# Two parts of a weight matrix requested from ScalarE's queue instead of SyncE's, in a block attention and gated MLP kernel

## The chip, the cores and the metric

The kernel runs on one core of a Trainium2 chip. A core has five engines that run side by side and meet through semaphores: TensorE (PE in the profile, PEld for its weight loads), VectorE (DVE), ScalarE (ACT), GpSimd (POOL) and SyncE (SP, here a pure issuer of transfers). The metric is the device time of one execution in microseconds. The kernel before took 508.56 us (median of 3 runs, 508.21 to 508.85).

## The reference, cut to what matters

```python
# block attention: B, H, S, D = 8, 8, 576, 64, in chunks of 64 positions
scores = scale * np.matmul(q_c, k_c.transpose(0, 1, 2, 4, 3))
scores = scores - np.max(scores, axis=-1, keepdims=True)
attn = np.exp(scores)
attn = attn / (np.sum(attn, axis=-1, keepdims=True) + 1e-09)
out = np.matmul(attn, v_c)
# gated MLP on x of [8, 576, 512]; w_in is [512, 1024], w_sg [576, 576], w_out [512, 512]
h = gelu_tanh(x @ w_in)
u, v = h[..., :512], h[..., 512:]
v_n = (v - mean(v)) / sqrt(var(v) + 1e-6) * g_ln
v_s = np.einsum('ts,bsd->btd', w_sg, v_n) + b_sg[None, :, None]
return x + (u * v_s) @ w_out
```

The weights `w_in` and `w_out` reach the kernel as 64-bit floating point words, and each is split on the chip into a high and a low part for the matrix products.

## The kernel before, in words

The 4,608 tokens are cut into 36 tiles of 128. For each tile the attention runs in three steps: S (scores on PE, maximum on DVE, exponentials on ACT, normalisation), T (transposition) and O (the product with v). The MLP then runs by batch element in units: v (the second half of w_in, gelu, the normalisation), u (the first half of w_in), s (w_sg), o (w_out). Each product is three matmuls of high and low parts.

The start is a list written out by hand, `START`. Its first steps are `L0 A0 L1 A1 L2 L3 A4 W0 S0 W1 D8 w0 S1 W2 T0 w1 ...`. L is `v_w_load`, the request of one of the four parts of w_in's second half (512 KB each, called `wsg_106`, `wsg_111`, `wout_115` and `wout_117` by the tiles whose memory they borrow). A requests attention tiles up to that number: tile 0 in two transfers, q and k together (512 KB) and v (256 KB), the later ones in one of 768 KB. W and w are the two halves of a part's conversion into high and low. W (`pair_begin`) is an absolute value on ACT (L130), then steps on DVE (L131, L132, L133, L162, L166). w (`pair_end`) is a negated copy to `win_h` on ACT (L174), five matmuls on PE (L178), which take the identity matrix `ident` and two scaled copies of it, `low`, as operands, and a copy to `win_l` on ACT (L179). D8 (`keep_clock`) is eight matmuls of `ident` with itself whose result nobody reads; each stands in the profile as two records. `ident` is cast on ACT (L103) from `eye`, which GpSimd makes, and the two `low` tiles are made from `eye` on ACT (L108).

The list is not the order on an engine. The framework schedules: it gives each engine one fixed order of its instructions, worked out from its own assumed durations, and on the chip each engine runs this order, waiting at each instruction until its operands are there. A transfer that an engine requests stands in that engine's order as well.

Lines of the kernel before that the prediction names: L291 and L292 request tile 0, L200 and L206 parts of w_in, L314 are the scores, L333 and L340 the maximum and its scaling, L344 tile 0's eight exponentials by head, L355 to L358 the normalisation, L366 the transposition, L398 the product with v, L97 a low part on DVE or GpSimd, L452 the v unit's matmuls, L577 those of D8. Behind the changed place the lines of the changed kernel have numbers one higher.

Of the kernel before, what the change touches and what calls it, by code (L numbers as in the profile page):

```python
# [25 lines left out]
DH = DF // 2  # L26
# [54 lines left out]
def block_attention_gated_mlp(ctx: ExitStack, tc: tile.TileContext, qkv, w_in, w_out, w_sg, g_ln, b_sg, out):  # L81
    nc = tc.nc
# [99 lines left out]
    def w_out_tile(i, dt=F32R):  # L182
        return const.tile([P, KT * DM], dt, name=f"wout_{i}", tag=f"wout_{i}")

    def w_sg_tile(i, dt=F32R):
        return const.tile([P, 5 * S], dt, name=f"wsg_{i}", tag=f"wsg_{i}")
# [10 lines left out]

    def v_w_load(kt):
        st = staged["v", kt] = w_sg_tile(kt, I32) if kt < 2 else w_out_tile(kt - 2, I32)
        nc.sync.dma_start(out=st[:, : 2 * DH], in_=w_in[:, kt, 2 * DH :])  # L200

    def u_w_load(dt):

# [351 lines left out]
    def att_slots(b, n):  # L555
# [9 lines left out]

    steps = {
        "L": v_w_load, "M": lambda k: load_misc(), "W": v_w_begin, "w": v_w_end, "X": u_w_begin, "x": u_w_end, "A": ahead,
        "S": att_scores, "T": att_transpose, "O": att_out, "P": lambda t: att_scores(t, t + 1), "Q": lambda t: att_out(t, t + 1),
    }
# [67 lines left out]
```

## Time and profile before

| what | value |
|---|---|
| median of 3 runs | 508.56 us |
| the profiled execution, its own time | 508.83 us |
| its span, first to last instruction | 507.0 us |
| granted clock of TensorE, mean | 0.998 |
| PE busy | 494.4 us (97%) |
| DVE busy | 339.1 us (67%) |
| ACT busy | 274.7 us (54%) |
| first matmul starts | 5.80 us |

The times of instructions count from the first instruction of the span. The time of an execution is 1.8 us more than the span. Busy time of PE is modelled from pipelined matmuls; a busy PE isn't PE at its peak. In a row of the timeline stand the start, the duration, the engine, the line, the operation, what it writes and reads, and in brackets how long the engine had been idle and what ended this. SPq and ACTq are the engines' issuing of transfers.

### The profile page before, as it was taken

The page shows a single profiled execution, that of the slowest core. Times are in us where ns is not written, and L with a number is a line of the kernel's source. Part 1 is how long each engine was busy: PE and PEld are TensorE (multiplying, and loading weights), DVE is VectorE, ACT ScalarE, POOL GpSimd, SP SyncE. Part 2 cuts the span into 40 slices and gives each one's busy share as a digit, 9 for nine tenths or more (in the row PEclk, how much of TensorE's full clock was granted, in tenths as well). Part 3 has the DMA queues.
Part 4 walks back from the last instruction along what each step waited for, and adds up shares of the span by engine and source line. Part 5 has one row for each costly group of instructions (what it writes and reads, how often), then busy time and mean ns, then how long its engine had stood idle before and what let it go on. Part 6 is the DMA issues. An engine that isn't in the chain of part 4 may idle for free.

```text
span 507.0 us, 12386 instructions
## 1 busy us (share of the span) xinstructions
PE 494.4 (97%) x5244; PEld 458.1 (90%) x5244; DVE 339.1 (67%) x707; ACT 274.7 (54%) x509; POOL 69.9 (14%) x72
## 2 busy tenths in 40 slices
PE   5999999999999999999999999999999999999996
PEld 4667898799999899989999899999999899999996
DVE  7998779888856947586563866576565676536141
ACT  5899667753445764355642775355643766334210
POOL 0112100210211401022100321022100141002000
PEclk9999999999999999999999999999999999999999
DMA  8948010228167204241324204060415200010002
GB/s 335 326 136 234 3 35 25 69 78 207 34 186 227 64 11 117 86 134 39 89 66 154 63 1 127 37 183 2 125 26 170 87 1 4 25 71 0 1 1 93
DMA packets 49595, 46.58 MB, mean 92 GB/s; under 512 B 35202, under 2 KB 39554, under 8 KB 49540
## 3 DMA queue, kind: packets, MB, share of 16 engines
q1 hardware_dynamic: 49540, 45.80, 30.3%
q8 instruction: 41, 0.67, 0.6%
q14 instruction: 14, 0.11, 0.1%
HBM read 36.34 MB, written 9.44 MB: 90 GB/s over the span
## 4 chain that ended last, share of the span: by engine, by line
PE 88%; DVE 6%; ACT 4%; DMA 1%; issue 1%; POOL 0%; DVEq 0%; SPq 0%; ACTq 0%
PE pm L509 21%; PE pm L489 20%; PE pm L532 19%; PE pm L452 18%; PE banks L322 3%; PE pm L410 3%; PE pm L178 2%; ACT pt L344 1%; DMA qkv_t<-qkv 1%; PE pm L314 1%; PE pm L577 1%; DVE gl L97 1%; DVE gt L513 1%; ACT L455 1%; DVE blocks L372 1%
## 5 line engine op out<-in xcount | busy, mean ns | idle before, releaser
L509 PE MATMUL pm<-wsg,v 128*128 128x288 f32 x768 | 107.9, 296 | 0.0
L509 PEld LDWEIGHTS pm<-wsg,v 128*128 128x128 f32 x768 | 103.9, 189 | 0.3
L532 PE MATMUL pm<-gh,wout 128*128 128x288 f32 x512 | 92.3, 297 | 0.0
L532 PEld LDWEIGHTS pm<-gh,wout 128*128 128x128 f32 x512 | 76.1, 189 | 0.5
L461 POOL TENSOR_TENSOR sm<-sm,neg_half 128x1 f32<-128x1 f32 x36 | 36.5, 1013 | 165.6 <-DVE sm L460 165.6
L358 POOL TENSOR_TENSOR pt<-pt,den 128x512 f32<-128x512 f32 x27 | 29.7, 1113 | 202.4 <-DVE den L357 128.0
L94 ACT CAST gh<-gt 128x576 fp32r<-128x576 f32 x32 | 21.5, 673 | 63.2 <-DVE gt L513 63.2
L532 PE MATMUL pm<-gl,wout 128*128 128x288 f32 x256 | 55.4, 296 | 0.0
L489 PE MATMUL pm<-xh,win_l 128*128 128x288 f32 x256 | 55.3, 298 | 0.0
L489 PE MATMUL pm<-xh,win_h 128*128 128x288 f32 x256 | 55.0, 296 | 0.0
L489 PE MATMUL pm<-xl,win_h 128*128 128x288 f32 x256 | 55.0, 296 | 0.0
L452 PE MATMUL pm<-win_h,xl 128*128 128x512 f32 x128 | 51.5, 402 | 1.4 <-DVE xl L97 0.9
L452 PE MATMUL pm<-win_l,xh 128*128 128x512 f32 x128 | 50.8, 397 | 0.0
L452 PE MATMUL pm<-win_h,xh 128*128 128x512 f32 x128 | 50.8, 396 | 0.0
L513 DVE TENSOR_TENSOR gt<-pm,u 128x576 f32<-128x576 f32 x32 | 24.1, 754 | 38.9 <-PE pm L509 38.9
L540 DVE TENSOR_TENSOR ot<-pm,xf 128x576 f32<-128x576 f32 (+1 forms) x33 | 24.1, 733 | 29.8 <-PE pm L532 29.7
L489 PEld LDWEIGHTS pm<-xh,win_l 128*128 128x128 f32 x256 | 41.4, 188 | 1.0
L532 PEld LDWEIGHTS pm<-gl,wout 128*128 128x128 f32 x256 | 41.4, 189 | 0.0
L489 PEld LDWEIGHTS pm<-xl,win_h 128*128 128x128 f32 x256 | 41.1, 188 | 0.0
L489 PEld LDWEIGHTS pm<-xh,win_h 128*128 128x128 f32 x256 | 41.0, 188 | 0.0
L97 DVE TENSOR_TENSOR xl<-pm,xh 128x512 fp32r<-128x512 f32 (+1 forms) x34 | 21.8, 641 | 26.2 <-ACT xh L94 26.2
L458 DVE BATCH_NORM_STATS2 sm<-hs 128x6 f32<-128x512 f32 x36 | 24.8, 689 | 20.9 <-ACT hs L455 20.7
(121 smaller groups left out, 820.0 us busy)
## 6 DMA issues: line engine op xcount, KB each, us to landing
qkv_t<-qkv SPq DMA_DIRECT2D x32, 512.0 KB, 4.6
out_dram<-ot SPq DMA_DIRECT2D x31, 288.0 KB, 2.2
qkv_t<-qkv SPq DMA_DIRECT2D x124, 64.0 KB, 3.7
qkv_t<-qkv SPq DMA_DIRECT2D x3, 768.0 KB, 11.9
wsg<-w_in SPq DMA_DIRECT2D x4, 512.0 KB, 6.1
wout<-w_in SPq DMA_DIRECT2D x4, 512.0 KB, 4.2
st<-w_out SPq DMA_DIRECT2D x8, 256.0 KB, 2.7
stage<-w_sg SPq DMA_DIRECT2D x5, 288.0 KB, 4.0
```

The costliest lines, as they stand in the source:

```text
L94: nc.scalar.copy(hi, src)
L97: lo_eng.tensor_tensor(lo, src, hi.bitcast(F32), op=ALU.subtract)
L322: nc.tensor.matmul(sc[o, c, h // 2, :], qt[r, 0, h, :], qt[r, 1, h, :], start=True, stop=True)
L358: (nc.gpsimd if t > last[1] else pick(f"n{t}")).tensor_tensor(pt, pt, den.unsqueeze(2).broadcast_to([P, H, D]), op=ALU.mult)
L452: nc.tensor.matmul(pv, a[:, kt, tok], c[:, kt, DH:], start=(i == 0), stop=(i == 11))
L458: nc.vector.bn_stats(st, h)
L461: nc.gpsimd.tensor_tensor(rs, rs, neg_half, op=ALU.pow)
L489: nc.tensor.matmul(pm[:, j, :HS], a[:, kt, dc], c[:, kt, j * HS : (j + 1) * HS], start=(i == 0), stop=(i == 11))
L509: nc.tensor.matmul(pm[:, j, :HS], a[:, dc], c[:, m, j * HS : (j + 1) * HS], start=(i == 0), stop=(i == len(ops) - 1))
L513: nc.vector.tensor_tensor(gt.rearrange("p (a c) -> p a c", a=2), pm[:, :, :HS], u2[0][:, dt, :].rearrange("p (a c) -> p a c", a=2), op=ALU ...
L532: nc.tensor.matmul(pm[:, j, :HS], a[:, kt, ec], c[:, kt, j * HS : (j + 1) * HS], start=(i == 0), stop=(i == len(ops) - 1),)
L540: nc.vector.tensor_tensor(ot[:, js], pm[:, js, :HS], res[:, js], op=ALU.add)
```

## The change

The first two of the four requests of w_in's second half (L0 and L1 of the list) go to ScalarE's queue. The other two, and all other transfers, stay with SyncE.

```diff
     def v_w_load(kt):
         st = staged["v", kt] = w_sg_tile(kt, I32) if kt < 2 else w_out_tile(kt - 2, I32)
-        nc.sync.dma_start(out=st[:, : 2 * DH], in_=w_in[:, kt, 2 * DH :])
+
+        (nc.scalar if kt < 2 else nc.sync).dma_start(out=st[:, : 2 * DH], in_=w_in[:, kt, 2 * DH :])
```

Since the framework schedules anew, instructions move on four engines over the first stretch of the program, up to the middle of the first batch element's units; behind that the orders are the same. On SyncE the first rows before were:

```order
L200 DMA wsg_106<-w_in 128x1024
L291 DMA qkv_t<-qkv 128x1024
L292 DMA qkv_t<-qkv 128x512
L200 DMA wsg_111<-w_in 128x1024
L294 DMA qkv_t<-qkv 128x1536
```

Now tile 0's q and k stand first, then its v and tile 1. On ScalarE, from the program's start, before:

```order
L130 ACT_TABLE_LOAD
L130 ACTIVATE wsg_106<-wsg_106 128x512
L174 ACTIVATE win_h<-wsg_106 128x512
L103 CAST ident<-eye 128x128
L108 ACTIVATE low_86<-eye 128x128
L108 ACTIVATE low_87<-eye 128x128
L130 ACTIVATE wsg_111<-wsg_111 128x512
L344 ACTIVATE pt,den<-pm,nmax 128x64 x8
```

On ScalarE now:

```order
L201 DMA wsg_106<-w_in 128x1024
L201 DMA wsg_111<-w_in 128x1024
L130 ACT_TABLE_LOAD
L130 ACTIVATE wsg_106<-wsg_106 128x512
L130 ACTIVATE wsg_111<-wsg_111 128x512
L345 ACTIVATE pt,den<-pm,nmax 128x64 x6
L103 CAST ident<-eye 128x128
L108 ACTIVATE low_86<-eye 128x128
L108 ACTIVATE low_87<-eye 128x128
L345 ACTIVATE pt,den<-pm,nmax 128x64 x2
L174 ACTIVATE win_h<-wsg_106 128x512
```

The absolute value of the second part and six of tile 0's exponentials now stand ahead of the cast of `ident`; the copy of the first part stands behind the exponentials. On VectorE, behind the seven memsets at the program's start, before:

```order
L131 TENSOR_SCALAR wsg_106<-wsg_106 128x512
L132 TENSOR_SCALAR wsg_106<-wsg_106 128x512
L133 SCALAR_TENSOR_TENSOR wsg_106<-wsg_106 128x512
L162 TENSOR_SCALAR wsg_106<-wsg_106 128x512
L333 TENSOR_REDUCE nmax<-pm 128x8
L166 SCALAR_TENSOR_TENSOR wsg_106<-wsg_106 128x512
L340 TENSOR_SCALAR nmax<-nmax 128x8
L131 TENSOR_SCALAR wsg_111<-wsg_111 128x512
```

On VectorE now, at the same place:

```order
L334 TENSOR_REDUCE nmax<-pm 128x8
L341 TENSOR_SCALAR nmax<-nmax 128x8
L131 TENSOR_SCALAR wsg_106<-wsg_106 128x512
L132 TENSOR_SCALAR wsg_106<-wsg_106 128x512
L131 TENSOR_SCALAR wsg_111<-wsg_111 128x512
L133 SCALAR_TENSOR_TENSOR wsg_106<-wsg_106 128x512
L132 TENSOR_SCALAR wsg_111<-wsg_111 128x512
L162 TENSOR_SCALAR wsg_106<-wsg_106 128x512
```

Tile 0's maximum and its scaling went ahead of all steps on w_in. The first rows of TensorE, tile 0's scores, D8 and the first part's matmuls (L178), stand as before.

## The prediction, made before the changed kernel had run

> **What bounds the kernel now.** I read the page's shares first, then the stretches, then the chain of waits and who waited for whom at the start, and last the start instruction by instruction. From the page:
>
> ```profile
> span 507.0 us, 12386 instructions
> PE 494.4 (97%) x5244; PEld 458.1 (90%) x5244; DVE 339.1 (67%) x707; ACT 274.7 (54%) x509; POOL 69.9 (14%) x72
> ```
>
> Busy time in stretches: the columns are PE, PEld, DVE, ACT, POOL, then the granted clock, the DMA share and GB/s.
>
> ```profile
> 0.00:5.00 5.00, 0.00 (x0) 0.00 (x0) 2.97 (x7) 1.76 (x2) 0.69 (x6) 1.00 0.63 209
> 5.00:10.00 5.00, 4.20 (x42) 4.06 (x43) 4.10 (x9) 2.70 (x11) 0.00 (x0) 1.00 1.03 411
> 11.00:38.30 27.30, 25.79 (x322) 17.31 (x320) 24.98 (x54) 24.35 (x72) 3.55 (x3) 1.00 0.74 244
> 38.30:60.00 21.70, 21.65 (x151) 16.84 (x154) 18.72 (x40) 17.58 (x34) 5.67 (x5) 1.00 0.49 135
> 80.00:90.00 10.00, 8.88 (x110) 7.84 (x110) 9.84 (x23) 6.61 (x13) 0.00 (x0) 1.00 0.16 49
> 90.00:100.00 10.00, 9.72 (x45) 7.64 (x44) 8.15 (x21) 9.12 (x19) 1.86 (x2) 1.00 0.22 61
> ```
>
> PE sets the time: of 507.0 us it stands idle 12.6, and 5.8 of these are the start. Up to 38.3 PE, DVE and ACT are all nearly full (PE 25.79 of 27.30), behind that PE alone is (21.65 of 21.70). So whatever makes PE later by 38 us stays, unless one of its few waits gives it back. The chain of waits, and what PE waited for up to 60 us:
>
> ```profile
> 1.17 4.58 DMA qkv_t<-qkv
> 5.80 1.97 PE pm L314 x32
> 7.77 3.30 PE pm L577 x16
> ...
> PE pm L314 <- DMA qkv_t<-qkv: 5.8, 1, 5.8
> PE pm L452 <- DVE xl L97: 0.9, 1, 0.9
> PE banks L398 <- ACT ptT L368: 0.4, 1, 0.4
> PE pm L452 <- POOL xl L97: 0.2, 1, 0.2
> ```
>
> So the chain begins with tile 0's q and k, then tile 0's scores (L314), then the filler step D8 (L577). Three waits of 1.5 us together are all that PE could make up between 11 and 60 us. The start in order of time:
>
> ```profile
> 0.73 0.39 SPq L200 DMA_DIRECT2D wsg<-w_in  x1
> 1.17 0.42 SPq L291 DMA_DIRECT2D qkv_t<-qkv  x1
> 4.52 0.66 ACT L130 ACTIVATE wsg<-wsg 128x512 f32<-128x512 f32 x1 [2.51 <-DMA wsg<-w_in]
> 5.21 0.43 DVE L131 TENSOR_SCALAR wsg<-wsg 128x512 f32<-128x512 f32 x1 [0.75 <-ACT wsg L130]
> 5.67 0.43 DVE L132 TENSOR_SCALAR wsg<-wsg 128x512 int32<-128x512 int32 x1
> 6.13 0.69 DVE L133 SCALAR_TENSOR_TENSOR wsg<-wsg 128x512 int32<-128x512 int32 x1
> 6.86 0.43 DVE L162 TENSOR_SCALAR wsg<-wsg 128x512 int32<-128x512 int32 x1
> 7.40 0.28 ACT L103 CAST ident<-eye 128x128 fp32r<-128x128 f32 x1
> 7.73 3.15 PEld L577 LDWEIGHTS pm<-ident 128*128 128x128 f32 x16
> 7.73 3.34 PE L577 MATMUL pm<-ident 128*128 128x128 f32 x16
> 7.82 0.69 DVE L333 TENSOR_REDUCE nmax<-pm 128x8 f32<-128x512 f32 x1 [0.53 <-PE pm L314]
> 8.43 0.68 DVE L166 SCALAR_TENSOR_TENSOR wsg<-wsg 128x512 uint16<-128x512 uint16 x1
> 9.03 0.17 DVE L340 TENSOR_SCALAR nmax<-nmax 128x8 f32<-128x8 f32 x1
> 9.29 0.31 ACT L344 ACTIVATE pt<-pm,nmax 128x64 f32<-128x64 f32 x1 [0.62 <-DVE nmax L340]
> ...
> 10.91 1.02 PE L178 MATMUL pm<-wsg,ident 128*128 128x512 f32 x2
> 11.05 0.34 ACT L344 ACTIVATE pt<-pm,nmax 128x64 f32<-128x64 f32 x1
> 12.25 0.69 DVE L358 TENSOR_TENSOR pt<-pt,den 128x512 f32<-128x512 f32 x1
> 13.62 0.42 PEld L366 LDWEIGHTS banks<-ident,pt 128*128 128x128 f32 x4
> 13.74 0.69 DVE L333 TENSOR_REDUCE nmax<-pm 128x8 f32<-128x512 f32 x1 [0.80 <-PE pm L314]
> ```
>
> See three things. ACT casts `ident` at 7.40, before tile 0's exponentials (9.29 on), and D8, which multiplies `ident`, starts 50 ns behind the cast's end, as the scores run out. DVE fills its wait for the scores with four steps on w_in's first part (5.21 to 7.29). And D8 ends at about 11, when w_in's first part has long been ready for L178 (L166 ends 9.11).
>
> **The change part by part.**
>
> *The two requests.* ACT issues two transfers ahead of its table load. One issue took SP 0.39 to 0.42; ACT has nothing to do until 4.52, so even 1 us each costs nothing. ACT's own issue cost isn't in this trace: it lies between this 0.4 and, as a far bound, the 2.5 us that ACT idles there. Cover gone, it would push the first Abs by its excess.
>
> *The landings.* From 5 to 10 us the transfers run at 411 GB/s with the engines full (1.03), so 512 KB take 524,288 / 411,000 = 1.28 us; the rows agree (w_in's part in by 4.52, q and k by 5.80). Two queues then share one full set of engines: q and k land between 4.5 (served first) and 5.8 (as now). Equal shares end both transfers near 5.8; I take 5.6. The next pair, v (256 KB, 0.64) and w_in's second part (1.28), is in by 5.8 + 1.9 = 7.7. The Trainium skill, "DMA: Bandwidth & Descriptors", section "Issuing engines are not separate DMA queues", speaks against the change: transfers from different engines' queues run on the same 16 DMA engines and interleave, and only the issue time is saved. By it q and k gain no more than the 0.44 us between the two issues above, and my 5.6 stands; served first they would have gained 1.3. No run here shows two queues at once.
>
> *The order on ACT.* Now the Abs of both parts stand first, then six of tile 0's eight exponentials, and only then `ident` and the two `low` tiles. So D8 waits for: q and k (5.6), the scores 1.97 (7.6), the maximum 0.69 and its scaling 0.17 (8.5, with 50 ns between engines), then a start at 8.6. The other branch, the second part at 7.7 and its Abs of 0.66, ends at 8.4 and just doesn't decide. Six exponentials take 11.05 - 9.29 = 1.76 (first start to seventh): 10.3. The cast, 0.28: 10.6. **D8 starts at 10.6, not 7.73: PE is 2.9 us late**, and idle from 7.6 to 10.6. If q and k come first, the Abs branch (second part third in line, 7.1, Abs 7.7) leaves +2.1; if they come last, more (below).
>
> *D8 itself.* Its 16 weight loads took 3.15 us, 0.197 each; four of the same shape at 13.62 took 0.42, 0.105 each, though the granted clock reads 1.00 in both. So D8 costs 3.3 again if PE is slow after standing idle, and 16 x 0.105 = 1.7 if not, 1.5 less. It is nearer to the old start, an idle PE, so I take 3.3. The Trainium skill, "TensorE: Matmul & The Clock Gate", section "Part 1: The HAM clock gate", has the array at half rate by default and after some 3.4 us of idleness, and at full rate after as much sustained work; by that 3.3 would stand only if 3 us idle are enough, and 1.5 us come off otherwise.
>
> *DVE.* The maximum of tile 0 now heads DVE's list, ahead of w_in's first part. DVE so idles from its last memset to 7.6, and 2.1 us of work (5.21 to 7.29) move behind the scores. From 8.5 it has two parts in full, 2 x (0.43 + 0.43 + 0.69 + 0.43 + 0.68) = 5.3, tile 0's normalisation of about 1.1, and five steps of the third and fourth part (four of 0.43, one of 0.69: 2.4): tile 1's maximum is reached at 17.3. PE delivers tile 1's scores for it at 13.74 + 2.9 = 16.6. So DVE isn't idle there, and against 13.74 it is 3.6 late with 2.4 of work done in advance: some 1.2 late in work. L166 of the first part ends near 12.8, before PE can use it.
>
> *What stays.* PE is 2.9 late; at most 1.5 comes back from its three waits. Of these the longest, 0.9, is for DVE, which is itself late by 1.2, so I let only 0.5 come back: **+2.4**. All later work is the same, and PE has no gap from 38.3 to 60. The sum stands against the profiled execution, 508.83 (span 507.0 and 1.8 around it): 511.2. The median of the runs lies 0.27 lower, so **511.0**.
>
> **The rivals.**
>
> A. *PE makes it up* (509.9; with a fast D8 as well 508.4; 509.3 for both together): all 1.5 of the waits vanish. For: D8 is filler whose end nobody but PE needs, and DVE is only 1.2 late. Against: the waits hang on DVE and ACT, which are late too.
>
> B. *The second part starves on its queue* (512.9 and more): if it lands behind tile 1's 768 KB too, that is 1.9 later, 9.6, its Abs ends at 10.3, and the exponentials, `ident` and D8 behind it in ACT's order move by 1.9: 511.0 + 1.9. Each further 512 KB ahead adds 1.28. For: SP holds seven transfers against ACT's two. Against: equal shares have it in by 7.7.
>
> C. *It gets faster* (506.3): q and k are served first (+2.1), D8 runs at the later pace (-1.5), and the new order removes PE's 1.5 of waits and the 1.4 that it idles from 80 to 100 us: -2.3. It decides once D8 ends before about 11.7 and most of these waits are gone. For: q and k head the chain. Against: three independent bits of luck; `ident` stays behind the exponentials.
>
> D. *It doesn't do what it says* (512.4): ACT's two transfers are served before q and k, which land at 4.5 + 2 x 1.28 = 7.1. Then `ident` comes 1.4 later still. Against: interleaving.
>
> **How the numbers follow.** Forecast 0.62 (own range 510.0 to 512.3), A 0.14, B 0.15, C 0.05, D 0.04. A measurement of this kernel can tell about 0.2%, 1.0 us, from no change. Slower takes the forecast, B, D and 0.05 of A: 0.86; same takes 0.09 of A; faster is C, 0.05. The range goes from 509.3 (the middle of A) to 513.3 (B with little behind it): outside lie C, the lower half of A and half of B, about 0.2.
>
> **What would show it.** ACT's two issues at 0.7 to 1.6, about 0.4 each. Tile 0's scores begin at 4.5 to 5.8 (right at 5.6). A new PE wait of about 3 us for ACT's `ident`, and D8 starting at 10 to 11: this is the heart of it. If D8 starts before 9 the forecast falls; after 12, B or D holds, told apart by whether the scores or the second Abs came late. D8's 16 loads take 3.15 or 1.7 in all. Tile 1's maximum starts at 16.5 to 17.5, DVE without a wait ahead of it. From 60 us on each step of PE is later by a constant 2 to 3 us; if that lag shrinks to under 1, A was right, and if it goes negative, C.

## The result and the profile after

The changed kernel takes 513.23 us (median of 4 runs, 513.12 to 513.69), the kernel before 508.42 us (median of 4 runs beside them, 508.21 to 508.85). The ratio is 1.0088, with a 95% interval of 1.0076 to 1.0100. It is slower by 4.8 us. The sign is the forecast's, but the loss is twice the forecast +2.4: the time lies 0.07 us inside the upper end of the wide range (513.3), which was set by rival B, and outside the forecast's own range (510.0 to 512.3). The profiled execution took 513.69 us, its span 511.9, which is 4.9 more than before. All times below that are not called a time of an execution count from the first instruction of a span. One execution of the run x5 below, 600.77 us at a granted clock of 0.757, is left out of its ratio.

The page of the changed kernel: span, busy time, and the new queue (ScalarE's is q10):

```profile
span 511.9 us, 12381 instructions
PE 495.1 (97%) x5239; PEld 458.9 (90%) x5244; DVE 336.7 (66%) x707; ACT 274.5 (54%) x509; POOL 69.4 (14%) x72
q10 hardware_dynamic: 288, 1.05, 0.5%
```

The span less PE's busy time was 12.6 us before; it is 16.8 now. So 4.2 of the 4.9 us are PE standing idle, and 0.7 is PE running longer. Where this lies shows in the stretches (columns as in the prediction):

```profile
5.00:10.00 5.00, 1.97 (x32) 1.78 (x32) 2.13 (x6) 2.07 (x8) 0.00 (x0) 1.00 1.03 421
11.00:38.30 27.30, 25.29 (x292) 18.58 (x295) 23.66 (x57) 23.00 (x71) 2.79 (x2) 1.00 0.79 250
38.30:60.00 21.70, 21.25 (x154) 16.06 (x156) 17.99 (x39) 16.52 (x32) 6.00 (x6) 1.00 0.42 125
```

From 5 to 10 us PE is busy 1.97 us instead of 4.20, and DVE 2.13 instead of 4.10, while the transfers run at the same full rate (421 GB/s against 411). From 11 to 38.3 us PE, DVE and ACT all do a little less than before. The waits of PE up to 60 us, and of DVE between 4.5 and 38.3 us:

```profile
PE pm L315 <- DMA qkv_t<-qkv: 5.8, 1, 5.8
PE pm L578 <- ACT ident L103: 3.5, 1, 3.5
PE pm L453 <- DVE xl L97: 1.7, 2, 1.3
PE banks L399 <- ACT ptT L369: 0.4, 1, 0.4
DVE nmax L334 <- PE pm L315: 7.0, 3, 3.3
```

A wait of 3.5 us for `ident` is new. PE's other waits behind the first scores have grown from 1.5 to 2.1 us. DVE stands idle 7.0 us in front of three maxima; before, the same group read 1.3 in two. The start in order of time:

```profile
0.72 0.89 ACTq L201 DMA_DIRECT2D wsg<-w_in  x2
...
5.79 1.97 PE L315 MATMUL pm<-qkv_t 64*64 64x64 f32 x32 [5.79 <-DMA qkv_t<-qkv]
5.95 0.66 ACT L130 ACTIVATE wsg<-wsg 128x512 f32<-128x512 f32 x1 [3.02 <-DMA wsg<-w_in]
7.81 0.69 DVE L334 TENSOR_REDUCE nmax<-pm 128x8 f32<-128x512 f32 x1 [3.35 <-PE pm L315]
8.59 0.67 ACT L130 ACTIVATE wsg<-wsg 128x512 f32<-128x512 f32 x1 [1.97 <-DMA wsg<-w_in]
9.17 0.29 ACT L345 ACTIVATE pt<-pm,nmax 128x64 f32<-128x64 f32 x1
10.90 0.32 ACT L103 CAST ident<-eye 128x128 fp32r<-128x128 f32 x1
11.27 3.78 PE L578 MATMUL pm<-ident 128*128 128x128 f32 x16 [3.51 <-ACT ident L103]
14.84 1.07 PE L178 MATMUL pm<-wsg,ident 128*128 128x512 f32 x2
17.71 0.69 DVE L334 TENSOR_REDUCE nmax<-pm 128x8 f32<-128x512 f32 x1 [1.61 <-PE pm L315]
25.48 0.69 DVE L334 TENSOR_REDUCE nmax<-pm 128x8 f32<-128x512 f32 x1 [2.00 <-PE pm L315]
```

Tile 0's scores start at 5.79 us, before at 5.80: q and k, now first on SyncE's queue, land no earlier. (Over all the traces the scores start at 5.6 to 6.0, with either queue.) The first part of w_in is in at 5.95 instead of 4.52, the second at about 8.55. ACT's list then runs as it is written: the second part's absolute value, six exponentials, `ident`, and D8 starts at 11.27 instead of 7.73. The chain that ended last now begins with the second part of w_in instead of q and k:

```profile
1.16 7.40 DMA wsg<-w_in
9.17 1.86 ACT pt L345 x12
11.27 3.78 PE pm L578 x16
```

The loss is made at the start. L178's first matmul is 3.9 us late (14.84 against 10.91), VectorE's first product with the s unit's result (`gt`) 4.5 (it starts at 75.78 against 71.27), and from there on the lag stays between 4 and 5 us.

### The profile page after: what moved, and what is told of

Same layout as the page of the kernel before. It is cut to its first block, busy times and chain, and to the rows that moved or that the text cites. A ratio compares the mean times of both kernels' runs of the same rounds, so it can differ in the third digit from the quotient of the medians.

```text
span 511.9 us, 12381 instructions
## 1 busy us (share of the span) xinstructions
PE 495.1 (97%) x5239; PEld 458.9 (90%) x5244; DVE 336.7 (66%) x707; ACT 274.5 (54%) x509; POOL 69.4 (14%) x72
## 4 chain that ended last, share of the span: by engine, by line
PE 83%; DVE 7%; ACT 4%; DMA 4%; issue 1%; POOL 1%; SPq 1%; ACTq 0%; DVEq 0%; POOLq 0%
PE pm L510 20%; PE pm L533 19%; PE pm L453 18%; PE pm L490 18%; PE banks L323 3%; PE pm L411 3%; DMA qkv_t<-qkv 2%; PE pm L178 1%; DMA wsg<-w_in 1%; POOL sm L462 1%; ACT pt L345 1%; PE pm L578 1%; DVE gl L97 1%; DVE gt L514 1%; DVE blocks L373 0%
```

## The experiments

The change does three things at once: it makes `ident` late, it makes w_in's first parts land later, and it gives VectorE and ScalarE another order. The theories are numbered so in the expectations: 1, the late `ident` is the loss; 2, the landings on the two queues are; 3 and later ones, the new order is, above all VectorE's, which lets it idle where it used to work. The runs were timed with those of the kernel before on the same chip; prices are the ratio's excess, taken of 509 us (for the change itself the medians of the first comparison lie 4.8 apart).

| run | edit | ratio, 95% interval | price, us | D8 starts | tile 1's maximum | PE idle in the span |
|---|---|---|---|---|---|---|
| before | | 1 | 0 | 7.73 | 13.74 | 12.6 |
| after | the change | 1.0088, 1.0076 to 1.0100 | +4.5 | 11.27 | 17.71 | 16.8 |
| e1 | after, `ident` by GpSimd | 1.0066, 1.0051 to 1.0081 | +3.4 | 7.61 | 15.82 | 15.0 |
| e2 | before, `ident` by GpSimd | 0.9998, 0.9984 to 1.0012 | -0.1 | 7.74 | as before | 12.8 |
| e3 | before, `ident` by VectorE, later | 1.0082, 1.0067 to 1.0097 | +4.2 | 9.40 | 17.0 | 15.9 |
| e4 | one part on ScalarE's queue | 1.0114, 1.0099 to 1.0129 | +5.8 | 11.23 | 17.87 | 18.6 |
| x1 | new queues, old order | 1.0047, 1.0030 to 1.0063 | +2.4 | 9.02 | 15.86 | 14.1 |
| x2 | old queues, new order | 1.0078, 1.0062 to 1.0095 | +4.0 | 10.76 | 17.54 | 16.1 |
| x3 | after, `ident` first | 1.0080, 1.0064 to 1.0096 | +4.1 | 7.73 | 15.94 | 15.6 |
| x4 | old queues and order, `ident` late | 1.0077, 1.0056 to 1.0099 | +3.9 | 11.61 | 18.38 | 16.5 |
| x5 | new queues, old order, `ident` first | 1.0000, 0.9991 to 1.0010 | 0.0 | 7.78 | 14.04 | 12.7 |
| x6 | before, D8 halved | 0.9982, 0.9974 to 0.9991 | -0.9 | 7.54 | 12.70 | 13.1 |
| x8 | before, `ident` first, tile 0's maximum ahead of w_in | 1.0046, 1.0029 to 1.0064 | +2.3 | 7.56 | 15.12 | 13.8 |
| x10 | old queues, old head, new tail | 1.0075, 1.0062 to 1.0087 | +3.8 | 7.59 | 15.40 | 15.9 |

### e1 and e2: `ident` off ScalarE's list

`ident` and `low` are made by GpSimd, in the changed kernel (e1) and, as a control, in the one before (e2).

```diff
-    nc.scalar.copy(ident_r, eye)
+    nc.gpsimd.tensor_copy(ident_r, eye)
...
-        nc.scalar.mul(a, eye, c)
+        nc.gpsimd.tensor_scalar(a, eye, c, None, op0=ALU.mult)
```

> The changed kernel, with the identity and the two scaled copies made on GpSimd from eye instead of on ACT, so that they no longer stand behind tile 0's exponentials. Theory 1 (the late identity): D8 starts right behind tile 0's scores, at about 7.8 instead of 11.27; D8 ends at about 11.1, the first part's third matmul then waits for DVE's L166 (12.3 in the changed kernel), so tile 1's maximum starts at 14.5 to 15 instead of 17.71, and the time is about 509.5 (a loss of 1 instead of 4.8). Theory 2 (the two queues: w_in's first part lands 1.4 later, the second about 1 later, whatever the identity does) and theory 3 (DVE's order, tile 0's maximum ahead of w_in): D8 starts early too, but the time stays at 512 to 513.

> Control: the kernel before, with the identity and its scaled copies made on GpSimd. All theories: D8 started 50 ns behind the cast and as the scores ran out, so nothing waits less; ACT is 0.8 us freer between 7.4 and 8.1, where it then waits for the maximum anyway. 508.0 to 508.7.

The control costs nothing (-0.1). In e1 D8 starts at 7.61, on time, and yet 3.4 of the 4.5 us stay. So taking away the late `ident`, the heart of the prediction, does not bring the loss back: something else then costs nearly as much.

### e3 and e4: the schedule answers to small edits

e3 casts `ident` in the kernel before as a step of the list, on VectorE behind tile 0's maximum. e4 sends only one of the two parts to ScalarE's queue.

```diff
-L0 A0 L1 A1 L2 L3 A4 W0 S0 W1 D8 w0 ...
+L0 A0 L1 A1 L2 L3 A4 W0 S0 I0 W1 D8 w0 ...
+    steps["I"] = lambda k: nc.vector.tensor_copy(ident_r, eye)
```

> The kernel before, all transfers on SyncE, but the identity is cast on DVE behind tile 0's maximum and its scaling, so late on purpose; the scaled copies stay on ACT. The cast should run at 9.2 to 9.5, D8 from 9.5 instead of 7.73: 1.75 late. Theory 1: PE's lag stays, and the time is 509.9 to 510.5. Theories 2 and 3: no transfer is touched and DVE gains only 0.3 of work, so 508.4 to 508.9.

```diff
-        (nc.scalar if kt < 2 else nc.sync).dma_start(...)
+        (nc.scalar if kt == 0 else nc.sync).dma_start(...)
```

> Only w_in's first part goes to ACT's queue; the second stays with SyncE. The identity now stands behind seven of tile 0's exponentials, but no longer behind the second part's Abs. Theory 1: scores end at 7.8 as before, exponentials from 8.7, the identity at about 10.9 and D8 from 11: 3.2 late, and the time is 511.5 to 513. Theory 2 (the second part's late landing is what costs): the time falls to 509.5 to 510.5.

In e3 D8 is only 1.7 us late, but the price is 4.2. The framework had scheduled anew and given PE nearly the changed kernel's order, and VectorE too from tile 0's normalisation on (its head stayed as before), though no request had moved. e4, half of the change, costs more than the whole (5.8). Neither tells causes apart; both say that what has to be held still is the order. All later kernels therefore fix it: behind the program stands a table of the instructions of each engine in the wanted order, and each is tied to the one ahead of it by an edge that makes no wait on the chip.

```diff
+    for row in ORDER.values():
+        names = ["I-" + n for n in row.split()]
+        for a, b in zip(names, names[1:]):
+            tc.add_manual_dep(now[b], a, DependencyInfo(NoSync, DATA), reason="order")
```

Their line numbers are 32 or 33 higher than those of the kernels they come from.

### x1 to x4: queues, order and `ident` apart

x1 is the changed kernel, held to the order before; x2 the kernel before, held to the changed order. x3 and x4 move only `ident` and `low` on ScalarE: to the head of the changed kernel's list, and behind the sixth exponential of the list before.

```diff
 ScalarE's row of the table, x3 (the changed kernel)
-requests, L130 L130 L345 x6, L103 L108 L108, L345 x2 ...
+requests, L103 L108 L108, L130 L130 L345 x8 ...
 ScalarE's row of the table, x4 (the kernel before)
-L130 L174 L103 L108 L108 L130 L344 x8 ...
+L130 L174 L130 L344 x6, L103 L108 L108, L344 x2 ...
```

> The changed kernel's queues (two parts of w_in on ACT), with the order of every engine held to that of the kernel before. Theory 2 (the two queues themselves cost): 511.5 to 513. Theory 4 (new, from the first four runs: the loss lies in the schedule's other order from tile 1's product to the first v units, whatever set it off): the time comes back to 508.4 to 509.5; some of it may stay, since w_in's first part lands 1.4 later here and the identity stands behind its negated copy, so D8 starts at about 9.2. Theory 1 (a late identity is passed on in full): 1.5 late, 509.9.

> The kernel before's queue (all on SyncE, w_in's first part, then q and k, as before), with the order of ACT, DVE and PE held to that of the changed kernel. Theory 2: 508.4 to 509.5. Theories 1 and 4: the loss is there without the queue, 512 to 513.3; D8 at about 10.7, behind six exponentials.

> The changed kernel with its order held, but for the identity's cast and the two scaled copies, which go to the head of ACT's order. Theory 1: D8 at 7.8, and the time falls to 509 to 510. Theory 4: D8 at 7.8 too, but the loss stays for the most part, 512 to 513, since the order behind is the same.

> The kernel before with its order held, but for the identity's cast and the two scaled copies, which go behind the sixth of tile 0's exponentials, where the changed kernel has them. D8 starts at about 11.4, 3.6 late. Theory 1: 511.5 to 512.5. Theory 4: at most 1 of the 3.6 is passed on, 508.4 to 509.5.

The four prices, 2.4, 4.0, 4.1 and 3.9 us, do not add to 4.5. The new order, with the late `ident` that belongs to it, costs 4.0 on the old queues (x2). The late `ident` alone costs 3.9 in the old order (x4), so the mechanism predicted is real; D8 is 3.9 late there, and tile 1's maximum 4.6. But with the new order and `ident` on time (x3) the price is 4.1 again. The causes overlap: each one alone costs nearly the whole. PE's and DVE's waits in x4 (two lines), then PE's in x3 (three lines):

```profile
PE pm L610 <- ACT ident L136: 3.6, 1, 3.6
DVE nmax L366 <- PE pm L347: 5.2, 2, 4.7
```

```profile
PE banks L400 <- DVE pt L392: 2.2, 1, 2.2
PE pm L486 <- DVE xl L130: 1.3, 2, 0.9
PE pm L211 <- DVE wsg L199: 0.6, 1, 0.6
```

In x4 PE waits for `ident`. In x3 it does not; it waits for VectorE instead, mostly for the normalised exponentials of tile 1 (`pt`). x1 left one thing unclear. Its `ident` stood in its old place on ScalarE, behind the copy of w_in's first part, which now lands later, so that D8 came at 9.02:

```profile
PE pm L611 <- ACT ident L136: 1.4, 1, 1.4
DVE wsg L164 <- ACT wsg L163: 2.0, 1, 2.0
DVE nmax L367 <- PE pm L348: 2.0, 1, 2.0
```

Whether its 2.4 us come from the landings or from this remaining delay of `ident` was for x5 to tell.

### x5: only the landings are left

x1, with `ident` and `low` cast first on ScalarE.

```diff
 ScalarE's row of the table
-requests, L130 L174 L103 L108 L108 L130 L344 x8 ...
+requests, L103 L108 L108 L130 L174 L130 L344 x8 ...
```

> The changed queues; every engine is held to the order of the kernel before, except that the identity and its two scaled copies are cast first on ScalarE. So of the change only the later landings are left (first part of w_in 5.95 us instead of 4.52, second 8.55). Theory 2 (the landings cost only what VectorE idles more before tile 4's maximum): D8 starts at 7.7 us, tile 0's maximum at 8.5, VectorE's idle time before tile 4's maximum 3.6 to 4.2 us (before 2.9), tile 4's maximum at 27.6 to 28.2 us (before 26.86), time 0.7 to 1.3 us over the kernel before. Theory 1 (all is the identity): D8 is on time, so within 0.5 us of the kernel before. The rival (the landings alone cost what the run with the new queues in the old order showed): 2.1 us or more over the kernel before, tile 4's maximum at 28.9 or later.

The price is 0.0 us (-0.5 to +0.5). The requests on ScalarE's queue and the later landings cost nothing that can be measured; of x1's 2.4 us all came with `ident` standing behind the copy, which starts D8 1.2 us later than here (9.02 against 7.78). That the price is more than the delay has a part in PE's slow pace at the start, which lasts longer in x1: D8 takes 3.78 us against 3.60, and the next two matmuls (L178's first, here L211) 1.47 against 1.02, so that tile 1's maximum is 1.8 later. My expectation, 0.7 to 1.3, was a miss on the high side. D8's start, and VectorE's waits:

```profile
7.78 3.60 PE L611 MATMUL pm<-ident 128*128 128x128 f32 x16
...
DVE wsg L164 <- ACT wsg L163: 2.3, 1, 2.3
DVE nmax L367 <- PE pm L348: 0.2, 1, 0.2
```

VectorE now waits 2.3 us for the first part of w_in. Before, it waited 0.8 for it and 1.3 for scores, 2.1 together: the later landing only moves its idle time ahead, and what it then works on is ready without a wait. Tile 1's maximum is 0.3 us later.

### x8 and x10: which part of the new order

Both keep the old queues and have `ident` in time. x8 takes one thing from the new order: tile 0's maximum and its scaling ahead of w_in's first part on VectorE. x10 keeps the order before on ScalarE and VectorE up to tile 0's normalisation, and has the new order behind it, and on PE and SyncE all through.

```diff
 VectorE's row of the table, x8, behind the memsets
-L131 L132 L133 L162 L333 L166 L340 ...
+L333 L340 L131 L132 L133 L162 L166 ...
```

> The queues of the kernel before and its order, with two changes: the identity first on ScalarE, and on VectorE tile 0's maximum and its scaling ahead of the first part of w_in instead of behind it (one part of the new order alone). VectorE then idles from about 4.5 to 7.7 us before that maximum, since the scores are ready only then. Theory 4 (VectorE's added idle time is the loss): about 2.1 us of idle time more there, less the 0.5 to 1.3 us of later waits that it takes along, so tile 4's maximum at 27.6 to 28.5 us (before 26.86) and the time 0.8 to 1.6 us over the kernel before. Theory 1 (the late identity is the loss): D8 is on time (7.7 us), so within 0.5 us of the kernel before.

> The queues of the kernel before; ScalarE and VectorE in the order before up to tile 0's normalisation (19 and 22 instructions), and behind that, and on PE and SyncE all through, in the order of the changed kernel. The identity is thus on time (D8 at 7.7 us), and tile 0's maximum stands behind the first part of w_in as before. If the head of the new order holds the whole loss: within 0.5 us of the kernel before, tile 4's maximum not later than 27.4 us. If the tail holds part of it (steps on the later parts of w_in ahead of tile 1's normalisation on VectorE, for which PE's transposes then wait): 1.5 to 3 us over the kernel before, tile 4's maximum at 28.4 to 30 us, and PE waits of about 2 us for tile 1's normalised exponentials.

x8's one exchange of place costs 2.3 us, more than the 0.8 to 1.6 expected. VectorE's wait at tile 0's maximum is the 3.2 us that was foreseen, and PE now waits for tile 0's normalised exponentials, which it transposes at 15.34:

```profile
DVE nmax L366 <- PE pm L347: 3.2, 1, 3.2
PE banks L399 <- ACT wout L163: 1.3, 1, 1.3
```

```profile
14.51 0.69 DVE L391 TENSOR_TENSOR pt<-pt,den 128x512 f32<-128x512 f32 x1
15.34 0.63 PE L399 MATMUL banks<-ident,pt 128*128 128x128 f32 x4 [1.27 <-ACT wout L163]
```

The profile puts that wait down to ScalarE, but VectorE's product, of which PE takes the result, ends at 15.20, 2.3 us later than before (12.25 + 0.69). The 2.3 us of price are not all this wait. Three of x8's six executions took 510.5 to 511.2 us, 1.3 to 2.0 above the median of the kernel before (509.16), with a granted clock of 1.000; the other three took 512.4 to 513.1 with 0.996 or 0.997. So the exchange itself is nearer to the expectation than the median says, and in half of the executions lost clock comes on top.

x10 costs 3.8 us, more than the 1.5 to 3 expected, so the tail of the new order has nearly the whole loss in it as well. (x10 moves the tail on ScalarE and VectorE and the order on PE together; they were not tried apart.) PE's waits, the rows around the longest of them, and PE's stretches there:

```profile
PE banks L399 <- DVE pt L391: 3.0, 1, 3.0
PE pm L485 <- DVE xl L130: 1.3, 2, 0.9
...
18.86 0.56 PE L347 MATMUL pm<-qkv_u 64*64 64x64 f32 x10
20.10 1.59 POOL L130 TENSOR_TENSOR xl<-xf,xh 128x512 fp32r<-128x512 f32 x1 [18.80 <-ACT xh L127]
20.48 1.77 DVE L391 TENSOR_TENSOR pt<-pt,den 128x512 f32<-128x512 f32 x1
22.39 0.86 PE L399 MATMUL banks<-ident,pt 128*128 128x128 f32 x4 [2.97 <-DVE pt L391]
23.18 1.54 PE L347 MATMUL pm<-qkv_u 64*64 64x64 f32 x22
24.76 0.69 DVE L366 TENSOR_REDUCE nmax<-pm 128x8 f32<-128x512 f32 x1 [2.52 <-PE pm L347]
...
22.40:24.60 2.20, 2.20 (x26) 1.80 (x26) 0.00 (x0) 1.77 (x5) 0.00 (x0) 0.55 0.92 306
24.60:26.80 2.20, 2.20 (x6) 0.75 (x4) 2.01 (x5) 0.59 (x2) 0.00 (x0) 0.67 0.11 37
```

Against these, two rows of the kernel before:

```profile
18.55 0.69 DVE L358 TENSOR_TENSOR pt<-pt,den 128x512 f32<-128x512 f32 x1
19.44 0.60 PE L366 MATMUL banks<-ident,pt 128*128 128x128 f32 x4
```

In the new order tile 1's transposition stands amid tile 3's scores on PE: 10 of the 32 matmuls of `qkv_u` ahead of it, 22 behind. Tile 1's normalisation ends at 22.25 (before 19.24), PE waits 3.0 us for it with 22 matmuls of the scores behind the wait, and VectorE in turn waits 2.5 us for these scores. Then PE pays a second time: behind the gap its granted clock is 0.55 and 0.67, so that 2.2 x 0.45 + 2.2 x 0.33 = 1.7 us of work are lost. The sum is PE's waits behind the first scores, 3.0 + 1.3 + 0.4 less 1.5 as before, +3.2; the clock, +1.7; D8, which took 2.7 here instead of 3.3, -0.6; together +4.3. The span has grown by 4.4, and PE's busy time (495.5 us against 494.4) bears out the last two, 1.7 less 0.6. D8's 0.6 is not the edit's: where nothing waits ahead of it, D8 took between 2.7 and 3.8 in the traces here.

e1 and x3 have the same clock gap (0.50 from 24.6 to 26.8 us in both); by the same working, from 22.4 to 30 us, it costs 1.7 us in each. after, x2 and x4, where `ident` is late and PE's gap lies ahead of D8, read 1.00 in these stretches. So the late `ident` and the new tail do not add: with `ident` late, PE comes to tile 1's transposition later, and its operand is ready by then. The same two steps in the changed kernel:

```profile
22.80 0.68 DVE L359 TENSOR_TENSOR pt<-pt,den 128x512 f32<-128x512 f32 x1
23.95 0.66 PE L367 MATMUL banks<-ident,pt 128*128 128x128 f32 x4
```

The normalisation ends at 23.48, and PE takes it up at 23.95 without a wait.

### x6: does the start pass on a gain too

The kernel before, held to its own order, with four of D8's eight matmuls (fewer results that nobody reads).

```diff
-L0 A0 L1 A1 L2 L3 A4 W0 S0 W1 D8 w0 ...
+L0 A0 L1 A1 L2 L3 A4 W0 S0 W1 D4 w0 ...
```

> The kernel before, held to its own order, with four instead of eight matmuls of D8 (their result is read by nobody). L178's operands are there at about 9.2 us while D8 ends at about 11; VectorE waits 0.8 us for tile 1's scores. If D8's end bounds the start and PE's clock does not need its second half: tile 1's maximum 0.8 us earlier (12.9 instead of 13.74), the time 0.8 us less than before. If the clock then comes later and matmuls stay at their slow pace: no gain or up to 1 us more. This measures whether what stands late on PE at the start is passed on in both directions.

Tile 1's maximum starts at 12.70, 1.0 us earlier (0.2 of it because this execution's scores started earlier), and the median falls by 0.9 us (0.9982, 0.9974 to 0.9991), as expected if D8's end bounds the start. That is just under the 0.2% at which a change of this kernel can be told by one comparison of a few runs; here 11 runs stand against 23. The profiled execution, with a span of 507.0, was the longest of the 11. It is the fastest version run. x5 with a halved D8 was not tried.

## Why the prediction was right, and where its size was wrong

*The requests* were right: ACT's two took 0.89 us together, beside idle time.

*The landings* were half right. q and k were taken at 5.6 and came at 5.79: of the 0.44 us that they could gain at most, they gained 0.01. The second part of w_in was taken at 7.7 and landed at about 8.55. This moves the branch that decides: not the maximum but the second part's absolute value (8.59) holds up the exponentials.

*D8's start* was the right mechanism with a size too small: 11.27 instead of 10.6, so +3.5 instead of +2.9. The landing just named gives some 0.35 of the difference (the first exponential starts at 9.17; in e4, where the second part's absolute value does not stand ahead of it, at 8.82), the scores' start at 5.79 instead of 5.6 another 0.2.

*D8's duration* was right in its choice, the slow pace, and a little low: 3.78 instead of 3.3. In all six runs where PE waits 1.4 us or more for `ident` it is 3.78; without a wait it is 2.70 to 3.78. That the idle time made PE slow is not shown, since x8 has 3.78 without any.

*What comes back*: here the prediction failed. "I let only 0.5 come back" of PE's three waits, but these grew from 1.5 to 2.1. The sum by its own terms is 3.5 (start) + 0.4 (D8) + 0.6 (waits) = 4.5, against 2.9 - 0.5 predicted and 4.9 of span measured; 0.4 are not located. The signs that the prediction named were overshot alike: D8 at 10 to 11 (11.27), tile 1's maximum at 16.5 to 17.5 (17.71), a lag of 2 to 3 us (4 to 5).

*VectorE*: "So DVE isn't idle there" was wrong. Work was taken as 17.3 us to tile 1's maximum and the scores as 16.6; measured, VectorE was through at 16.1 and the scores came at 17.7. Two parts worked on in turn go faster than the sum of their durations, as three neighbouring steps of VectorE in the changed kernel show:

```profile
9.06 0.43 DVE L132 TENSOR_SCALAR wsg<-wsg 128x512 int32<-128x512 int32 x1
9.41 0.42 DVE L131 TENSOR_SCALAR wsg<-wsg 128x512 f32<-128x512 f32 x1
9.74 0.68 DVE L133 SCALAR_TENSOR_TENSOR wsg<-wsg 128x512 int32<-128x512 int32 x1
```

Steps of 0.42 us start 0.33 to 0.35 apart here, while the steps of one part in the prediction's rows (5.21, 5.67, 6.13) start 0.46 apart. So VectorE gives up 2.1 us of work under the first scores, and reaches tile 1's maximum too early all the same, since PE, held up by `ident`, has not made the scores.

*The cause*: the forecast made `ident` the cause. In the changed kernel it is what PE waits for (3.5 us), and it is a sufficient cause (x4, +3.9), but e1 and x3 show that it is not a needed one: with `ident` in time the kernel would still have been slower, so that the sign did not hang on it. The prediction costed the new order as a mere displacement of work. x8 (+2.3) and x10 (+3.8) show that its head and its tail each cost by themselves, and x5 (0.0) that with the order held the transfers cost nothing. So the loss comes by way of the new schedule, in which a late `ident` and a worse order of VectorE and PE are alternatives that hide each other. Whether the later landings add anything within the new order is open: D8 starts 0.5 later in the changed kernel than in x2 (11.27 against 10.76), but their prices, 4.5 and 4.0, have intervals that overlap.

*The rivals*: A (PE makes it up) and C fell: no wait was given back. B had a grain of truth, the second part 0.85 later than equal shares had it. Its time, 512.9, is nearer to the measured one than the forecast's, but by luck: the landing at 9.6 that it rests on did not happen (8.55). D fell: q and k were not pushed back.

## What to carry to other kernels

Where a scheduler fixes the order, a moved request is first of all a new order: hold the old order by edges without a wait and the move can be priced alone (here 0.0 us), and then decide on the order by itself. Ask of each engine that runs its list strictly in order what stands behind its first wait; one reduction ahead of four steps that were ready cost 2.3 us in the median here. And taking away the longest wait of a trace can price it too low (1.1 us came back in e1, while a late `ident` alone costs 3.9 in x4): when several waits cover each other, undoing each alone, in both kernels, is what tells them apart.

## What the runs showed of the hardware that was not expected

The granted clock falls in the middle of the work after short gaps. In x10 PE stood idle for 3.0 us ahead of 22.39 and then ran at 0.55 and 0.67 for 4.4 us; in x3 a wait of 2.2 us within a stretch that was half idle (1.67 us busy of 3.4) was followed by 0.50. The Trainium skill, "TensorE: Matmul & The Clock Gate", section "Part 1: The HAM clock gate", gives half rate after at least one idle window of about 3.4 us. The direction agrees, but here less idleness was enough. A wait of 1.5 us (e3, at 36.62) left the clock at 1.00 in the stretches behind it. At the start this column does not show the slow pace: D8's 16 weight loads took 3.48 us in the changed kernel with the granted clock at 1.00, 0.22 each, where four of the same shape take 0.42 at 17.59, 0.105 each.

A VectorE product took 1.77 us beside a GpSimd subtraction and 0.69 without one: in x10 the subtraction runs from 20.10 to 21.69, the product starts at 20.48 and ends at 22.25, 0.56 behind it. The Trainium skill, "SBUF — State Buffer", section "SBUF: two separate sides", says that the two engines share a port pair that one of them holds for a whole instruction; the rows agree. This adds 1.1 us to the wait of PE that costs x10 most; x3 and e1 have the same (1.75 and 1.76 us). In the changed kernel the product starts first (22.80, ahead of the subtraction at 23.16) and takes 0.68.
